# Second layer of the first two token groups in seven products instead of eight, two of them ahead of group 1's first layer

## The chip, the core and the metric

The kernel runs on one core of a Trainium2 chip. The metric is the device time of one execution in microseconds (us). TensorE (PE) multiplies matrices, VectorE (DVE), ScalarE (ACT) and GpSimd (POOL) work on tiles in SBUF (and, but for POOL, in PSUM, where products are summed), and SyncE (SP) issues the DMAs.

## The reference

Everything is fp32: causal attention of 4 batches, 12 heads, 448 tokens and 64 values a head, whose output is the input of a two-layer network.

```python
scores = scale * np.matmul(q, k.transpose(0, 1, 3, 2))
scores = np.where(mask, -1000000000.0, scores)
scores = scores - np.max(scores, axis=-1, keepdims=True)
attn = np.exp(scores)
attn = attn / (np.sum(attn, axis=-1, keepdims=True) + 1e-09)
attn_out = np.matmul(attn, v)
...
x = np.ascontiguousarray(attn_out.transpose(0, 2, 1, 3)).reshape(B * S, H * D)
h = x @ w_in
relu6 = np.clip(h + 3.0, 0.0, 6.0)
g = h * relu6 / 6.0
return (g @ w_out).astype(np.float32)
```

x is 1792 x 768, w_in 768 x 2048 and w_out 2048 x 768.

## The kernel before

**Products.** To keep fp32 exactness, both factors of a product are split into a rounded high part and the remainder. ACT casts the high part (`wh`, `gh`, line 284), and DVE or POOL subtracts it to get the remainder (`wl`, `gl`, line 296). A 128 x 128 x 448 product is then three matmuls (`triple`, lines 668 to 670): high by high, high by low, low by high.

**Groups.** The 1792 tokens are four groups of 448. Group 0 holds the first 112 queries of every batch (`first_pair`, one call for each of 6 pairs of heads). The others are computed by `unit(g, p)`: q by k (line 507), maxima on DVE (line 555, each followed by a read of its accumulator), exp on ACT (line 562), normalisation by `prow` (lines 574, 575 and 582), transposes (line 594) with their copies (lines 284 and 287), and the product with v (line 529). In the first `N_RAW` = 7 units q and k go into PE as fp32; in the later ones they are split first.

**The network.** `group(g)` does groups 0 and 1. The first layer has 16 chunks of 128 hidden rows with 18 matmuls each. Line 697 gates a chunk, and its split into `gh` and `gl` (one buffer of all 16 chunks for each) follows at once. The second layer has 6 output tiles of 16 chunks by 3 matmuls, 576 matmuls for both groups. Group 0 also turns the weights (64-bit words) into fp32: three DVE bit operations (lines 642, 644, 647), twice 384 wide for a chunk of w_in and once 512 wide for one of w_out. The result is stored in DRAM (`kept`) for the later groups.

Groups 2 and 3 are multiplied together, with seven products of halves in place of eight (`last_first`, `last_second`). This needs sums of blocks of the weights (`sums4`, `last_sums`, stored in `kept_s`) and of the activations.

**Order.** Every operation is recorded with a due time (`T_*`, `flow.op`) and with the engines that may do it. `Flow.run` then goes through the work with a cost for each operation and writes down the order of every engine; buffers, banks and the turn on one SBUF port that DVE and POOL share in this model (`port`) hold operations back. On the chip each engine goes through its list in that order and waits on semaphores. The due times in question:

```python
T_FIRST, T_EARLY, T_EACH, T_LATE, T_DENSE, T_LOAD, T_W, T_WLOAD = -66, 8, 13, 84, 7, -24, 9, 9
t = T_EARLY + T_EACH * at if g == 1 else T_LATE + T_DENSE * (at - NPAIR)
```

Of the kernel before, what the change touches and what calls it, by code (L numbers as in the profile page):

```python
# [18 lines left out]
C = 112  # L19
# [209 lines left out]
def tile_causal_attention_hardswish_moe(ctx: ExitStack, tc: tile.TileContext, q, k, v, w_in, w_out, out):  # L229
# [47 lines left out]
    def elem(n, psum=False):  # L277
        return (n + 150) / 960
# [62 lines left out]
    def first_pair(p):  # L341
        t = T_FIRST + 7 * p
        for a, src in enumerate((q, k)):
            dma(
                -900 + 4 * p, 265e3, lambda a=a: by_batch(ap(first_qk)[:, 2 * p + a]),
                lambda src=src: src[:, p, :, :, :C].rearrange("b e d s -> (e d) b s"),
                w=[(first_qk, p, a)],
            )
        dma(
            -900 + 4 * p + T_V, 265e3, lambda: ap(first_v)[:C, p].rearrange("c (b m) -> c b m", b=B),  # L350
            lambda: v[:, p, :, 0].rearrange("b c e d -> c b (e d)"), w=[(first_v, p)],
# [16 lines left out]
        def products():  # L368
            qa, ka = (by_batch(ap(first_qk)[:, 2 * p + a]) for a in range(2))
# [7 lines left out]
        pe(t, [(1.1, products, keys)], [(first_qk, p, 0), (first_qk, p, 1)], True)  # L377
# [61 lines left out]
        def times_v():  # L439
            va = ap(first_v)[:C, p].rearrange("c (b e d) -> c b e d", b=B, e=2)  # L440
# [659 lines left out]
```

## Time and profile before

| | |
|---|---|
| time, median of 3 runs | 613.1 us (612.42 to 614.92) |
| the profiled execution | 614.25 us, span 612.5 us |
| mean granted clock of TensorE | 0.989 |
| PE busy | 599.6 us (98%) |
| DVE busy | 470.2 us (77%) |
| ACT busy | 365.9 us (60%) |
| POOL busy | 269.1 us (44%) |

The span runs from the first to the last instruction of the profiled execution; its own time is 1.75 us longer. A busy share is over the whole span, whose stages differ. A row's duration on PE and DVE can overlap the next row's, so the step from one start to the next is the cost of an instruction in a row of them.

### The profile page before, as it was taken

Reading aid. Unit: us, or ns where it says so; the run is one execution under the profiler, and the core shown is the slowest. Engines: PE = TensorE matmul, PEld = TensorE weight load, DVE = VectorE, ACT = ScalarE, POOL = GpSimd, SP = SyncE. Lnnn points to the kernel's source line nnn. Section 1 sums busy time; section 2 is a strip of 40 time slices with the busy share of each in tenths; the row PEclk is TensorE's granted clock in tenths of the full one; section 3 lists DMA queues with packets and bytes.
Section 4 is the critical chain, followed back from the end, with each engine's and each line's share of the span. In section 5 each row is a group of like instructions: output and inputs, shape, how many; then the busy total and the mean of one; then the engine's idle time right before and its main releaser. Section 6 shows DMA issues by size and latency. Waiting matters only on the chain.

```text
span 612.5 us, 11307 instructions
## 1 busy us (share of the span) xinstructions
PE 599.6 (98%) x3724; PEld 522.2 (85%) x3724; DVE 470.2 (77%) x1044; ACT 365.9 (60%) x846; POOL 269.1 (44%) x277
## 2 busy tenths in 40 slices
PE   7799999999999999999999999999999999999997
PEld 5577888887888888888888888899999999999996
DVE  5879987887796876688786755588778878898861
ACT  3955757655555767776576655375545575446630
POOL 1767785654676347655184161005554343010000
PEclk8979999999999999999999999999999999999999
DMA  9969986988898654444365344435554367583321
GB/s 207 258 176 331 336 270 229 331 254 287 262 289 255 196 172 143 138 137 142 109 173 166 118 127 133 126 117 176 166 167 162 121 196 241 164 261 114 116 68 54
DMA packets 79738, 114.68 MB, mean 187 GB/s; under 512 B 20736, under 2 KB 55488, under 8 KB 79680
## 3 DMA queue, kind: packets, MB, share of 16 engines
q1 hardware_dynamic: 79248, 113.80, 61.2%
q8 instruction: 29, 0.48, 0.3%
q14 instruction: 29, 0.24, 0.1%
q10 hardware_dynamic: 432, 0.17, 0.1%
HBM read 86.80 MB, written 27.13 MB: 186 GB/s over the span
## 4 chain that ended last, share of the span: by engine, by line
PE 92%; DMA 2%; DVE 2%; ACT 2%; POOL 1%; SPq 1%; issue 0%; DVEq 0%; POOLq 0%
PE b L668 24%; PE b L669 23%; PE b L670 23%; PE b L594 7%; PE b L507 7%; PE b L529 7%; DMA gh<-in_k_dram 1%; SPq L275 1%; DMA wd<-in_w_in_dram 1%; PE b L430 1%; ACT d L284 0%; PE b L373 0%; ACT d L392 0%; POOL d L582 0%; POOL d L421 0%
## 5 line engine op out<-in xcount | busy, mean ns | idle before, releaser
L668 PE MATMUL b<-d,wh 128*128 128x448 f32 x504 | 187.4, 372 | 1.0 <-DVE r L697 1.0
L669 PE MATMUL b<-d,wh 128*128 128x448 f32 x504 | 182.9, 363 | 0.0
L670 PE MATMUL b<-d,wl 128*128 128x448 f32 x504 | 182.2, 361 | 0.0
L284 ACT CAST wh<-wd 128x768 fp32r<-128x768 f32 (+1 forms) x92 | 71.5, 778 | 59.1 <-PE b L669 35.2
L668 PEld LDWEIGHTS b<-d,wh 128*128 128x128 f32 x504 | 94.7, 188 | 10.0 <-DVE r L697 1.4
L670 PEld LDWEIGHTS b<-d,wl 128*128 128x128 f32 x504 | 94.4, 187 | 7.0 <-POOL wl L296 0.3
L669 PEld LDWEIGHTS b<-d,wh 128*128 128x128 f32 x504 | 94.8, 188 | 5.0
L555 DVE CUSTOM_DVE_ANT_0 b<-b,mask 112x448 f32<-112x448 f32 (+2 forms) x144 | 69.5, 533 | 29.8 <-PE b L507 29.1
L296 DVE TENSOR_TENSOR wl<-wd,wh 128x768 fp32r<-128x768 f32 (+1 forms) x67 | 59.9, 894 | 32.3 <-ACT wh L284 31.4
L668 PE MATMUL b<-gh,wh 128*128 128x448 f32 x192 | 74.6, 388 | 0.0
L296 POOL TENSOR_TENSOR wl<-d,wh 128x512 fp32r<-128x512 f32 (+1 forms) x38 | 58.5, 1540 | 30.0 <-ACT wh L284 28.7
L670 PE MATMUL b<-gh,wl 128*128 128x448 f32 x192 | 69.7, 363 | 0.0
L669 PE MATMUL b<-gl,wh 128*128 128x448 f32 x192 | 69.7, 363 | 0.0
L296 POOL TENSOR_TENSOR wl<-wd,wh 128x768 fp32r<-128x768 f32 (+1 forms) x25 | 43.5, 1741 | 59.1 <-DVE vr L948 43.5
L284 ACT COPY d<-b 112x336 f32<-112x336 f32 (+2 forms) x110 | 46.5, 454 | 35.5 <-PE b L594 22.1
L562 ACT ACTIVATE pr<-b,prow 112x336 f32<-112x336 f32 (+1 forms) x96 | 47.0, 497 | 9.6 <-DVE prow L555 6.3
L507 PE MATMUL b<-d 64*112 64x448 f32 (+2 forms) x376 | 46.7, 376 | 0.4 <-DVE prow L414 0.4
L582 POOL TENSOR_SCALAR pr<-pr,prow 112x224 f32<-112x224 f32 (+1 forms) x69 | 33.9, 503 | 29.3 <-DVE prow L575 19.7
L529 PE MATMUL b<-d,vr 112*64 112x224 f32 (+2 forms) x504 | 44.9, 329 | 0.0
L529 PEld LDWEIGHTS b<-d,vr 112*64 112x64 f32 x504 | 30.6, 137 | 15.6 <-issue 2.6
L296 POOL TENSOR_TENSOR d<-d 128x560 fp32r<-128x560 f32 (+3 forms) x19 | 28.0, 1473 | 35.9 <-PE b L507 18.3
L594 PE MATMUL b<-ident,pr 112*112 112x112 f32 x240 | 43.2, 262 | 0.0
(110 smaller groups left out, 1072.4 us busy)
## 6 DMA issues: line engine op xcount, KB each, us to landing
wd<-in_w_in_dram SPq DMA_DIRECT2D x32, 384.0 KB, 5.9
wd<-in_w_out_dram SPq DMA_DIRECT2D x24, 512.0 KB, 5.4
wd<-kept_w SPq DMA_DIRECT2D x32, 384.0 KB, 3.5
wd<-kept_w SPq DMA_DIRECT2D x84, 128.0 KB, 3.1
kept_w<-d SPq DMA_DIRECT2D x16, 384.0 KB, 6.5
kept_w<-d SPq DMA_DIRECT2D x24, 256.0 KB, 5.4
wd<-kept_w SPq DMA_DIRECT2D x24, 256.0 KB, 2.8
kept_s<-wd SPq DMA_DIRECT2D x12, 512.0 KB, 3.5
```

Source lines behind the costliest of these rows:

```text
L275: flow.op(key, {queue: (1, 0)}, [(0.1, lambda e: start(out=o(), in_=i()), w)], r, nbytes=nbytes)
L284: nc.scalar.copy(o(), i()) if scale is None else nc.scalar.mul(o(), i(), scale)
L296: (nc.gpsimd if e == "P" else nc.vector).tensor_tensor(o(), a(), b(), op)
L507: nc.tensor.matmul(ap(ps[e, i])[:C, :w], x[m, c], y[m, nq:nq + w], start=n == 0, stop=n == len(terms) - 1)
L529: nc.tensor.matmul(ap(av)[64 * e:64 * e + 64, off + nq - w:off + nq], ap(vr)[:, j, e, :], ap(ph)[:, e, o:o + w], start=(j == 0), stop=(j = ...
L555: lambda _, e=e, i=i, w=w, dst=dst, st=st: nc.vector.tensor_tensor_reduce(dst(), dst(), mask[:, S - w:], -0.125, 3.0e38, ALU.add, ALU.min, ...
L562: lambda _, e=e, i=i, dst=dst, st=st, pr=pr: nc.scalar.activation(row_of(pr, e, i), dst(), ACTF.Exp, bias=ap(st)[:, e, i:i + 1], scale=-1. ...
L582: (nc.gpsimd if w == "P" else nc.vector).tensor_scalar(x, x, ap(st)[:, e, 4 + i:5 + i], 1.0, ALU.mult, ALU.mult)
L594: nc.tensor.transpose(ap(tp)[:C, C * o:C * o + C], row_of(pr, e, i)[:, C * j:C * j + C], ident)
L668: nc.tensor.matmul(ps, ap(wh)[:, a], xh, start=start, stop=False, skip_group_check=more)
L669: nc.tensor.matmul(ps, ap(wh)[:, a], xl, start=False, stop=False, skip_group_check=more)
L670: nc.tensor.matmul(ps, ap(wl)[:, a], xh, start=False, stop=stop, skip_group_check=more)
```

## The change

- The second layers of groups 0 and 1 are done together by `mid_second` as seven products of 72 matmuls (504 in all). Products 1 and 2 need only group 0 and stand ahead of group 1's first layer; the other five follow it.
- The hidden values stay whole, in tiles of two chunks. `factors` makes totals and the high and low parts anew for each product, 896 wide. The sums of the weights' blocks are made earlier (`T_SUMS` 86 in place of 190).
- w_out is turned in calls of its own (`turned`, `T_OUT`), and its parts are made 768 wide from `kept`.
- Attention is due earlier (`T_EARLY`, `T_EACH`, `T_LATE`, `T_DENSE`), `N_RAW` is 9, the cost of an elementwise operation in the planner is smaller, and the pools `gh` and `gl` go into the pool `d` (38 tiles of 3.5 KB a partition in place of 22).

```diff
-T_FIRST, T_EARLY, T_EACH, T_LATE, T_DENSE, T_LOAD, T_W, T_WLOAD = -66, 8, 13, 84, 7, -24, 9, 9
-T_XA, T_X, T_LAST, T_PAIR, T_SUMS = 156, 178, 192, 10.5, 190
-N_RAW = 7
+T_FIRST, T_EARLY, T_EACH, T_LATE, T_DENSE, T_LOAD, T_W, T_WLOAD = -66, -2, 7, 40, 6.5, -24, 9, 9
+T_PRODUCT, T_PAIR = 12, 10.5
+T_GROUP = 0, 72
+T_MID = {1: 48, 2: 60, 6: 120, 7: 132, 4: 144, 5: 156, 3: 168}
+T_XA, T_X, T_LAST = 152, 168, 180
+T_OUT, T_SUMS, T_SUM = ((32, 2.5), (68, 2.5)), 86, 2.2
+N_RAW = 9
...
-    gh=1, gl=1, prow=4, r=4, kl=3, vr=3, wh=3, wl=3, pr2=3, pr1=3, wd=6, d=22,
+    prow=4, r=4, kl=3, vr=3, wh=3, wl=3, pr2=3, pr1=3, wd=6, d=38,
...
-        for m in range(NK):
-            acc, ob = bank("mo"), buf("r", [128, S])
-            for part in range(8):
...
-                    for i in (2 * part, 2 * part + 1):
-                        triple(
-                            ap(acc)[:, :n], n, wh, wl, i % 4, ap(gh)[:, i, :n], ap(gl)[:, i, :n], i == 0, i == NF - 1
-                        )
...
+    PLACE = {"11": (0, 0), "21": (0, HF), "12": (1, 0), "22": (1, HF)}
+    NAME = {1: "11", 2: "21", 6: "11", 4: "21", 7: "12", 5: "11", 3: "22"}
+
+    def factors(g, n, t0, lead=T_W + T_WLOAD):
...
+                wh, wl = parts_of(t - 6, 768, lambda wd=wd: ap(wd), [(wd, m) for m in range(HK)], HK)
+                c = 4 * hh + 2 * cc
+                ts = t0 + 1.5 * c
+                if n == 6:
+                    total(ts - 5, c, "12", "22", "12", ALU.subtract)
+                    total(ts - 4.9, c, "11", "12", "11", ALU.add)
+                elif n == 4:
+                    total(ts - 5, c, "21", "21", "11", ALU.subtract)
+                elif n == 5:
+                    total(ts - 5, c, "11", "22", "11", ALU.subtract)
+                v, (xh, xl) = gv(NAME[n], c), (buf("gt", [128, 2, S], F32R) for _ in range(2))
+                vk = [(v, 0), (v, 1)]
+                move(ts - 4.8, 2 * S, lambda xh=xh: ap(xh), lambda v=v: ap(v), vk, [(xh, 0)], {"A": 1.05})
+                minus(
+                    ts - 4.7, 2 * S, lambda xl=xl: ap(xl), lambda v=v: ap(v), lambda xh=xh: f(ap(xh)), vk + [(xh, 0)],
+                    [(xl, 0)], {"D": 1, "P": (1.87, .5)},
+                )
+                steps = [(ts + 1.5 * b, c + b, b, (xh, xl), wh, wl) for b in range(2)]
+                rows.append(steps)
+        return rows
...
+    def mid_second(g):
+        so, s1 = [buf("so", [128, 2, S]) for _ in range(HK)], [buf("kl", [128, S]) for _ in range(HK)]
+        for n, t0 in T_MID.items():
+            fresh = n in ((1, 6, 5) if T_MID[2] == T_MID[1] + T_PRODUCT else (1, 2, 6, 5))
+            if fresh:
+                X = [buf("m", [128, 512]) for _ in range(HK)]
+            for k, steps in enumerate(factors(g, n, t0, T_W + (4 if n < 3 else T_WLOAD))):
+                for ms in ([m] for m in range(HK)) if not k else [range(HK)]:
+                    row(steps, X, ms, not fresh)
...
+    for late, quarters in enumerate(((0, 1, 2, 3), (0, 2, 1, 3))):
+        for a, (x, m) in enumerate((x, m) for x in quarters for m in range(HK)):
+            t = T_OUT[late][0] + T_OUT[late][1] * a
+            turned(NF + 4 * (m + HK * late) + x, t, t - T_WLOAD)
...
-    last_sums()
+    weight_sums()
+    mid_second(both)
     last_second(last_first(last_x()))
```

The lines of the kernel after are some ten higher: a triple is at lines 676 to 678, q by k at 514, the product with v at 536, the transposes at 601, the bit operations at 640, 642 and 645, the gate at 688, the maxima at 562, a copy on DVE at 296, a subtraction or sum at 305 and a normalisation at 589.

The first place is on PE, where group 0's first layer ends. Before, transposes of attention lead into group 0's second layer, on the split hidden values `gh` and `gl`:

```order
L594 MATMUL b_1532<-ident_105,pr1_1360 112x112
L594 MATMUL b_1532<-ident_105,pr2_1303 112x112
L594 MATMUL b_1532<-ident_105,d_1212 112x112
L668 MATMUL b_1536<-gh_668,wh_1468 128x448
L669 MATMUL b_1536<-gl_686,wh_1468 128x448
L670 MATMUL b_1536<-gh_668,wl_1508 128x448
```

After, product 1 begins there, in three banks of which b_2112 is the first (b_2112 is also the first bank of product 2), on parts made by `factors` (d_705 high, d_772 low):

```order
L536 MATMUL b_2048<-d_2011,vr_1846 64x112 x4
L514 MATMUL b_2088<-d_1820 112x448
L514 MATMUL b_2090<-d_1820 112x448
L514 MATMUL b_2103<-d_1820 112x336
L514 MATMUL b_2105<-d_1820 112x336
L676 MATMUL b_2112<-d_705,wh_2063 128x448
L677 MATMUL b_2112<-d_772,wh_2063 128x448
L678 MATMUL b_2112<-d_705,wl_2079 128x448
```

On PE, 360 matmuls of triples stand from the first of the network to the first of product 2 (288 of group 0's first layer, 72 of product 1). Among them stand 64 q by k products (16 of 448 columns, 20 of 336, 28 of 224), 180 transposes, 86 products with v and 16 small matmuls of `first_pair`.

The second place is on DVE, about the middle of group 0's network. Before, bit operations on w_out (`wd`) stand between the maxima of attention:

```order
L642 TENSOR_SCALAR b<-wd 128x512
L644 SCALAR_TENSOR_TENSOR b<-wd,b 128x512
L647 SCALAR_TENSOR_TENSOR d<-wd,b 128x512
L555 ISA b,prow<-b,mask 112x448
L555 ISA prow 112x1
L642 TENSOR_SCALAR b<-wd 128x512
L644 SCALAR_TENSOR_TENSOR b<-wd,b 128x512
L647 SCALAR_TENSOR_TENSOR d<-wd,b 128x512
L555 ISA b,prow<-b,mask 112x448
```

After, four copies of transposed blocks (`d<-b`), gates and more maxima stand there as well:

```order
L296 COPY d<-b 112x336 x4
L688 SCALAR_TENSOR_TENSOR d<-r,b 128x448
L562 ISA b,prow<-b,mask 112x224
L562 ISA prow 112x1
L562 ISA b,prow<-b,mask 112x224
L562 ISA prow 112x1
L562 ISA b,prow<-b,mask 112x224
L562 ISA prow 112x1
L562 ISA b,prow<-b,mask 112x224
L562 ISA prow 112x1
L581 TENSOR_SCALAR prow<-prow 112x2x3
L582 RECIPROCAL prow<-prow 112x2x3
```

DVE's list for the stretch of PE just counted holds 30 times the three bit operations 384 wide (15 chunks of w_in) and 12 times those 512 wide, 16 gates, the 64 maxima that belong to the q by k products, 27 copies (17 of 336 columns, 5 of 224, 4 of 448, 1 of 112), 4 remainders 768 wide and 1 of 896, 5 normalisations, and 16 pairs of a small operation and a reciprocal on `prow`.

The third place is on POOL, around group 1's second layer. Before, normalisations and remainders of q and k and of w_out:

```order
L582 TENSOR_SCALAR d<-d,prow 112x448 x2
L296 TENSOR_TENSOR wl<-wd,wh 128x512
L296 TENSOR_TENSOR d<-d 128x784
L582 TENSOR_SCALAR pr_4842<-pr_4842,prow 112x224
L582 TENSOR_SCALAR pr_4817<-pr_4817,prow 112x336
L582 TENSOR_SCALAR d<-d,prow 112x448
```

After, totals and remainders of the hidden values, 896 wide, and sums of the weights (`wd<-wd`):

```order
L305 TENSOR_TENSOR d<-d 128x896
L305 TENSOR_TENSOR wd<-wd 128x256 x2
L305 TENSOR_TENSOR wl<-wd,wh 128x768
L305 TENSOR_TENSOR wd<-wd 128x256
L589 TENSOR_SCALAR d<-d,prow 112x448
L305 TENSOR_TENSOR d<-d 128x896 x6
```

In the whole program DVE and POOL go from no operation 896 wide to 72 and 25. For the stretch of PE from the chunk of group 1's first layer in bank b_3857 to the third quarter of product 7 in bank b_4633, the fourth product on PE (253 matmuls of triples, 110 transposes, 84 q by k products, 80 products with v), the lists of the two hold these operations on SBUF alone: DVE 18 of 896, 26 of 256, 9 of 768, 19 normalisations and 16 small ones; POOL 7 of 896, 10 of 256, 5 of 768, one of 784, two of 560 and 13 normalisations.

## Rows read from the trace of the kernel before

**Rows 1.** The page, parts 1 and 4: busy time and the chain that ended last.
```profile
PE 599.6 (98%) x3724; PEld 522.2 (85%) x3724; DVE 470.2 (77%) x1044; ACT 365.9 (60%) x846; POOL 269.1 (44%) x277
...
PE 92%; DMA 2%; DVE 2%; ACT 2%; POOL 1%; SPq 1%; issue 0%; DVEq 0%; POOLq 0%
```

**Rows 2.** Windows (us; PE, PEld, DVE, ACT, POOL busy; PEclk; DMA share; GB/s).
```profile
40.00:60.00 20.00, 19.01 (x99) 16.18 (x97) 17.00 (x42) 12.04 (x29) 14.42 (x13) 1.00 0.89 313
60.00:80.00 20.00, 20.00 (x127) 17.33 (x126) 19.00 (x49) 14.73 (x37) 16.40 (x16) 1.00 0.96 332
60.00:140.00 80.00, 80.00 (x488) 68.50 (x488) 68.57 (x166) 51.33 (x128) 54.82 (x54) 1.00 0.86 287
440.00:540.00 100.00, 100.00 (x501) 93.73 (x501) 82.31 (x144) 54.15 (x89) 38.70 (x32) 1.00 0.58 177
```

**Rows 3.** Timeline of PE (start us, us, engine, operation, count).
```profile
100.17 2.31 PE L529 MATMUL b<-d,vr 112*64 112x336 f32 x24
...
173.87 1.57 PE L507 MATMUL b<-d 64*112 64x448 f32 x8
...
184.62 1.20 PE L507 MATMUL b<-d 64*112 64x336 f32 x8
...
198.57 1.33 PE L507 MATMUL b<-d 64*112 64x448 f32 x12
...
207.12 1.02 PE L507 MATMUL b<-d 64*112 64x336 f32 x12
...
208.31 0.26 PE L594 MATMUL b<-ident,pr 112*112 112x112 f32 x1
208.41 0.26 PE L594 MATMUL b<-ident,d 112*112 112x112 f32 x1
```

**Rows 4.** Timeline of DVE, 70 to 113 us.
```profile
70.06 1.01 DVE L642 TENSOR_SCALAR b<-wd 128x384 int32<-128x384 int32 x2
...
72.84 0.61 DVE L697 SCALAR_TENSOR_TENSOR r<-r,b 128x448 f32<-128x448 f32 x1
...
88.98 0.63 DVE L555 CUSTOM_DVE_ANT_0 b<-b,mask 112x448 f32<-112x448 f32 x1 [1.16 <-PE b L507]
...
89.53 0.62 DVE L697 SCALAR_TENSOR_TENSOR r<-r,b 128x448 f32<-128x448 f32 x1
90.06 0.63 DVE L555 CUSTOM_DVE_ANT_0 b<-b,mask 112x448 f32<-112x448 f32 x1
...
98.80 0.43 DVE L555 CUSTOM_DVE_ANT_0 b<-b,mask 112x224 f32<-112x224 f32 x1
...
99.15 0.43 DVE L555 CUSTOM_DVE_ANT_0 b<-b,mask 112x224 f32<-112x224 f32 x1
...
110.00 0.69 DVE L642 TENSOR_SCALAR b<-wd 128x512 int32<-128x512 int32 x1
...
112.06 0.61 DVE L697 SCALAR_TENSOR_TENSOR r<-r,b 128x448 f32<-128x448 f32 x1
```

**Rows 5.** Groups of DVE instructions by shape (busy us, mean ns, idle before).
```profile
L296 DVE TENSOR_TENSOR wd<-wd 128x256 f32<-128x256 f32 x35 | 14.9, 457 | 0.9 <-DMA kept_s<-wd 0.9
...
L287 DVE COPY d<-b 112x336 f32<-112x336 f32 x21 | 10.3, 503 | 4.2 <-PE b L594 4.1
...
L296 DVE TENSOR_TENSOR d<-d 128x784 fp32r<-128x784 f32 x4 | 4.2, 1058 | 0.8 <-ACT wh L284 0.8
```

**Rows 6.** Groups of POOL instructions by shape.
```profile
L296 POOL TENSOR_TENSOR wl<-wd,wh 128x768 fp32r<-128x768 f32 x20 | 37.0, 1853 | 56.5 <-DVE vr L948 43.5 <-ACT wh L284 4.9 <-ACT d L284 2.3
...
L296 POOL TENSOR_TENSOR wd<-wd 128x256 f32<-128x256 f32 x13 | 9.5, 742 | 42.6 <-DVE wd L296 35.7 <-PE b L670 3.8 <-DVE wl L296 2.1
```

**Rows 7.** Timeline of POOL and DVE, 12 to 15 us.
```profile
12.02 1.83 POOL L421 TENSOR_TENSOR d<-d,prow 112x448 f32<-112x448 f32 x2 [10.15 <-DVE prow L414]
...
12.92 0.95 DVE L386 TENSOR_SCALAR prow<-prow 112x4 f32<-112x4 f32 x1
...
14.95 0.17 DVE L413 TENSOR_SCALAR prow<-prow 112x8 f32<-112x8 f32 x1
```

More of the change, by code (lines that the diff above doesn't have):

```diff
@@ L744, in halves @@
+                pe(t + part, [(6 * S * .4535e-3, products, [(acc, 0), ("step", t + part)])], [(wh, 0), (wl, 0)] + xs)
+            gated(t - 4, r, lambda acc=acc: ap(acc)[:, :S], (acc, 0), places[i // 2], i % 2)
+        return places
     def halves(key, x, o, v, r, ways):
@@ L774, in last_x @@
                 if h == 0:
-                    out(t, c, 1, at(0, c, 0))
-                    out(t + .2, c, 2, at(0, c, 1))
-        for k in range(5):
+                    both(t, c, (1, 2), x[0][c])
+        for k in range(3):
             for c in range(HK):
-                t = T_X + (c, 4 + c, 5.5 + c, 7 + c, 9 + c)[k]
+                t = T_X + (c, 4 + c, 5.5 + c)[k]
                 b11, b21, b12, b22 = (at(h, c, k) for h in range(2) for k in range(2))
@@ L819, in last_first @@
     def last_first(x):
-        g = [buf(a, [128, NF, S]) for a in ("gh", "gl")]
+        g = [hiddens() for _ in range(2)]
         for i in range(HF):
@@ new lines, in row, with products, store @@
+    def row(steps, banks, ms, adds):
+        def products(m):
+            for _, c, b, x, wh, wl in steps:
+                xh, xl = (ap(y)[:, b] for y in x)
+                triple(ap(banks[m])[:, :S], S, wh, wl, 2 * m + b, xh, xl, c == 0 and not adds, c == HF - 1, adds)
+        pe(
+            steps[0][0], [(len(steps) * 3 * .2013, lambda m=m: products(m), [(banks[m], 0)]) for m in ms],
+            [(y, 0) for x in steps for y in (x[4], x[5], *x[3])],
+        )
+    def store(key, g, m, o, v, queues=("SP", "SP")):
+        rows, at = by_batch(out[128 * m:128 * m + 128]), 0
+        if not g:
+            dma(key, 230e3, lambda: rows[:, :, :C], lambda: by_batch(v()), [o])
+        for (b, tiles, _), queue in zip(UNITS.get(g, ()), queues):
+            w, c = C * len(tiles), C * tiles[-1]
+            dma(
+                key, 512 * w, lambda rows=rows, b=b, c=c, w=w: rows[:, b, c:c + w],
+                lambda at=at, w=w: v()[:, at:at + w], [o], (), queue,
+            )
+            at += w
@@ L1018, in last_second @@
+            banks, rows = acc[n], factors(g, n, t0)
+            if n == 3:
+                for steps in rows[:2]:
+                    row(steps, banks, range(HK), True)
+                for m in range(HK):
+                    row([x for steps in rows[2:] for x in steps], banks, [m], True)
+            else:
+                for steps in rows:
+                    row(steps, banks, range(HK), n in (6, 7))
             t = t0 + 5
```

353 lines of the change are left out of this document (155 added, 198 removed).

## The prediction

> **What bounds the kernel now.** I read the page first: PE is busy for 599.6 of 612.5 us, and 92% of the chain that ended last is PE [rows 1]. DVE is next with 77%. So PE's own work sets the time, and a change is worth what it takes off PE, less what PE then waits for. The windows say where it waits: from 60 to 140 us PE is busy throughout, from 40 to 60 it loses 0.99 us while DVE is busy for 17.00 of 20 [rows 2]. The reader is to see two things there. A matmul taken off PE shortens the run by its full step only where nothing else is as close to the edge. And DVE is close to it early: 19.00 of 20 us from 60 to 80, 68.57 of 80 from 60 to 140, still without a wait on PE [rows 2].
>
> **What PE saves.** From 440 to 540 us PE does 501 matmuls of triples back to back in 100.00 us [rows 2], so one costs 0.1996 us. The second layers go from 576 to 504 matmuls: 72 x 0.1996 = 14.4 us less. `N_RAW` from 7 to 9 gives two units back to fp32 products. Such a unit takes 1.57 + 1.20 = 2.77 us on PE, one with split factors 1.33 + 1.02 = 2.35 [rows 3]: 2 x 0.42 = 0.84 us more. PE's net saving is 13.5 us. Moving products on PE is free in itself. It moves what the other engines owe them.
>
> **What it costs early, on DVE.** Attention is due earlier, but all of the weights' bit operations stay where they were, in group 0's network. The order gives both lists from the first matmul of the network to product 2.
>
> PE, in that stretch: 360 matmuls x 0.1996 = 71.9 us. The q by k products have 20,160 columns; the fp32 run of 1.57 us holds two of 448 and two of 336 columns, so 1.0 ns a column [rows 3], 20.2 us. Transposes start 0.10 us apart [rows 3]: 180 make 18.0. Twelve products with v (24 records) take 2.31 [rows 3]: 86 make 16.6. With 16 small ones at 0.10, 1.6, PE needs **128.3 us**.
>
> DVE, by the step from one start to the next [rows 4]: a chunk of w_in takes 72.84 - 70.06 = 2.78 us, 15 make 41.7. One of w_out takes 112.06 - 110.00 = 2.06, 12 make 24.7. A gate is 0.53, 16 make 8.5. A maximum with its read is 0.55 at 448 columns and 0.35 at 224, so about 0.45 at 336: 16, 28 and 20 make 8.8, 9.8 and 9.0. A 336-wide copy lasts 0.503 [rows 5], 0.41 as a step, since rows 4 overlap the next by some 0.09 us. With 0.54, 0.32 and 0.2 for the other widths, 27 make 11.0. Remainders 768 wide take about 0.95 (1.06 for 784 columns [rows 5], less the overlap), 5 with one of 896 make 4.9. Five normalisations at some 0.35, 1.8. Sixteen pairs of small operations, two at 0.17 [rows 7], 5.4. The sum is **125.6 us**, 98% of PE's.
>
> No row shows DVE kept at 98% by this mixture. With no gap it costs PE nothing. At the fullest slice's share, 0.95 [rows 2], DVE needs 125.6 / 0.95 = 132.2 us, 3.9 more than PE. At the average of 60 to 140, 0.857 [rows 2], it needs 146.6, or 18.3 more. In that average DVE had idle time that cost nothing, because its queue was short; here work is queued throughout. So I take **+4**, from the nearer row, 60 to 80. It can give back at most the 0.99 us that the kernel before loses from 40 to 60, since PE is busy throughout after that; I don't credit it.
>
> **What it costs late, on the port of DVE and POOL.** The hidden values' parts are now made again for each product, 896 wide, between SBUF tiles. Such operations of DVE and POOL keep each other out: while POOL works from 12.02 to 13.85 us, a DVE operation on 4 columns lasts from 12.92 to 13.87, where one on 8 columns takes 0.17 us a moment later [rows 7]. The Trainium skill's page "SBUF — State Buffer", section "Who interferes with whom", says that a VectorE instruction with two SBUF inputs and a GpSimd instruction that reads SBUF exclude each other for the whole instruction, as does a VectorE instruction in a two-port mode. By that rule the work below can't be laid side by side, and the sum is the +5 below; without it each engine alone fits under PE, and the sum is 0. The trace agrees with the rule in kind (0.95 against 0.17 us); how tightly the two can take turns it doesn't show.
>
> From group 1's chunk in b_3857 to the third quarter of product 7, PE has 253 x 0.1996 + 110 x 0.10 + 84/24 x 2.35 + 80/12 x 2.31 = 50.5 + 11.0 + 8.2 + 15.4 = **85 us**. DVE on SBUF alone, with 0.09 off each row's duration [rows 5]: 18 of 896 at 1.10 (784 columns take 1.06, so 896 about 1.19), 26 of 256 at 0.37, 9 of 768 at 0.95, 19 normalisations at no more than the 256-wide 0.37, 16 small ones at 0.14: 19.8 + 9.6 + 8.6 + 7.0 + 2.2 = 47. POOL: 1.85 for 768 columns and 0.74 for 256 [rows 6] give 2.13 for 896, 1.9 for 784 and 1.4 for 560; 7, 10 of 256, 5 of 768, one and two of those, and 13 normalisations at some 0.6 make 14.9 + 7.4 + 9.3 + 1.9 + 2.8 + 7.8 = 44. Together 91 us of 85. If operations on one engine hide wholly behind the other's, this costs 0, and no less, since PE had no wait to lose there. If the port is handed over without a gap, +6, and at a share of 0.95, +11. I take **+5**: some of the work can be done ahead, before the stretch. What is late then is the low part of a product's values, for which PE waits within products 6 and 7.
>
> **Other edits, costed at nothing.** The 36 more 128 KB loads of weights (84 to 120) and 16 more loads or stores of block sums, less the 256 KB ones of w_out, lie in or before the products, where the DMA share is about half (0.58 from 440 to 540 [rows 2]). Their cover is the lead of 13 to 18 us of due time before a product. If the early ones are late, PE waits at product 1; that is the rival on transfers. The larger pool `d` holds tiles that have no other claim. ACT has fewer operations and is at 60% [rows 1].
>
> **The sum.** The profiled execution: 612.5 - 13.5 + 4 + 5 = 608.0 us of span, and 1.75 more, as in its own time of 614.25, makes 609.8. That execution lies 1.15 above the median of 613.1 that the forecast is held against: 613.1 - 13.5 + 9 = **608.6**, say 608.5 us.
>
> **Rivals.**
> (a) All that PE saves is kept. DVE does its 125.6 us without a gap, and the port's work is spread ahead: 599.6 us, up to 602.5 with 3 us of waits. For it: PE never waits from 60 to 140 us, with DVE at 0.95 in a slice. Against it: both stretches would have to run fuller than any row.
> (b) The forecast: waits of 3 to 10.5 us together, 602.5 to 610.
> (c) The early stretch eats most of the saving: 610 to 616.2. DVE's share s decides. The saving left after the +5 is 8.5 us; 125.6 / s - 128.3 reaches it at s = 0.918. For it: from 40 to 60 us PE already waited while DVE was at 0.85 [rows 2], since a maximum or a gate can't start before its product.
> (d) Slower. The same place and mechanism, with DVE held at the share that it had on average: 18.3 us, 613.1 - 13.5 + 5 + 18.3 = 622.9. It is slower by over 0.5% below s = 0.898. For it: DVE's list is served in its written order, so a maximum that waits for its q by k products holds the bit operations queued behind it, and these are what group 0's next chunk on PE waits for. Against it: in that average PE didn't wait, so nothing pressed DVE.
> (e) Transfers, on the same side as (d). The DMA queues are at 0.96 from 60 to 80 us and at 0.86 over 60 to 140 [rows 2]. Up to 0.96 there is room for 0.10 x 80 = 8 us of transfers. If the q, k and v that are now due earlier need half as much again, 12 us by this estimate, PE loses 4 at the first units: 612.6. The stretch holds the weights' loads and stores that it held before, so I give it little.
>
> **How the numbers follow.** Chances: (a) 0.14, (b) 0.35, (c) with (e) 0.29, (d) 0.22. A measurement of this kernel tells some 0.5% from no change, 3.1 us: faster is below 610.0, slower above 616.2. Faster is (a) and (b), 0.49; the same (c), 0.29; slower (d), 0.22. The likeliest case alone runs from 602.5 to 610. The range is 600 to 621: it leaves out a few hundredths of (a), below 600, and the part of (d) at the average share and beyond, some 0.14.
>
> **What the profile will show.** PE's busy time on triples falls by 14.4 us, and q by k rises by 0.8. If the step on DVE is right, PE idles some 4 us between the first triples and product 2, ended by DVE's bit operations or gates, in slices where DVE is at 0.95 or more. If the step on the port is right, PE waits some 5 us within products 6 and 7 for a low part that DVE or POOL made, and DVE's and POOL's SBUF work together fills those slices. If instead PE idles for products of attention while DVE is at 0.86, (d) holds. I would be wrong in kind if PE waited on a DMA at product 1, or if short waits made the granted clock fall in a stretch where it is now 1.00 [rows 2], since each matmul there would then cost more than its 0.1996 us.

## The result and the profile after

The changed kernel takes 620.3 us (618.15 to 621.21, 4 runs) beside 612.9 for the kernel before: a ratio of 1.0109, 95% interval 1.0075 to 1.0144. It is slower by some 7 us where 4 faster were forecast. The profiled execution took 618.15 us, its span 616.4. It is the fastest of the four, where that of the kernel before (614.25) lies above its median, so the two spans differ by 3.9 us, some half of what the medians do. The page's busy times and chain, which answer to [rows 1]:

```profile
PE 594.1 (96%) x3636; PEld 511.2 (83%) x3636; DVE 516.8 (84%) x1039; ACT 352.7 (57%) x755; POOL 263.8 (43%) x252
...
PE 46%; DVE 12%; DMA 9%; SPq 3%; POOL 3%; issue 2%; ACT 1%; DVEq 0%; ACTq 0%; POOLq 0%
```

PE has 88 matmul records fewer, as the change says (72 of triples, 16 of two units back to fp32), but is busy for only 5.5 us less, and its idle time, span less busy, rises from 612.5 - 599.6 = 12.9 us to 22.3. PE made up 92% of the chain and now 46%; DVE, DMA and SyncE's queue (SPq) came in. The windows say where (columns as in [rows 2]); the four that answer to [rows 2], then three of 2 us, then the stretches from 40 us on:

```profile
40.00:60.00 20.00, 19.78 (x120) 15.82 (x119) 19.79 (x56) 15.54 (x40) 13.75 (x15) 1.00 0.92 317
60.00:80.00 20.00, 20.00 (x127) 15.24 (x127) 18.70 (x54) 12.39 (x32) 12.99 (x14) 1.00 0.90 315
60.00:140.00 80.00, 80.00 (x520) 62.68 (x519) 70.99 (x200) 49.41 (x133) 52.65 (x58) 1.00 0.81 262
...
440.00:540.00 100.00, 100.00 (x502) 93.75 (x501) 82.92 (x106) 55.09 (x79) 34.63 (x22) 1.00 0.29 87
...
144.00:146.00 2.00, 2.00 (x8) 1.11 (x7) 1.93 (x8) 0.64 (x2) 1.24 (x3) 0.54 0.35 135
146.00:148.00 2.00, 1.82 (x11) 1.35 (x10) 2.00 (x10) 1.30 (x5) 1.91 (x4) 0.50 0.46 103
148.00:150.00 2.00, 2.00 (x11) 1.44 (x11) 1.51 (x4) 2.00 (x7) 0.00 (x0) 0.50 0.83 223
...
40.00:140.00 100.00, 99.78 (x639) 78.50 (x638) 90.79 (x255) 64.95 (x172) 66.40 (x72) 1.00 0.84 273
140.00:200.00 60.00, 55.80 (x345) 43.26 (x344) 48.95 (x119) 32.91 (x83) 28.37 (x28) 0.94 0.80 243
200.00:280.00 80.00, 80.00 (x600) 67.04 (x600) 72.07 (x190) 53.97 (x141) 45.84 (x55) 1.00 0.89 278
280.00:420.00 140.00, 135.64 (x851) 119.31 (x852) 132.43 (x231) 80.79 (x150) 56.75 (x46) 1.00 0.66 205
```

The kernel before, in the two stretches that differ:

```profile
140.00:200.00 60.00, 60.00 (x377) 48.63 (x378) 46.60 (x112) 35.73 (x97) 37.24 (x42) 1.00 0.88 273
...
280.00:420.00 140.00, 139.79 (x967) 120.00 (x966) 99.61 (x242) 87.13 (x209) 49.85 (x60) 1.00 0.46 133
```

A matmul of a triple still takes 0.20 us (440 to 540). From 40 to 140 us PE loses 0.22 us, less than the 0.99 that the kernel before loses from 40 to 60 [rows 2], with DVE at 19.79 of 20 us in a slice. The new idle time is 60 - 55.80 = 4.20 us from 140 to 200, where the granted clock also falls to half, and 140 - 135.64 = 4.36 from 280 to 420 (before: 0 and 0.21).

The first loss, in the timeline of PE, DVE and SyncE's queue from 132 to 149 us:

```profile
132.01 0.69 DVE L645 SCALAR_TENSOR_TENSOR d<-wd,b 128x512 int32<-128x512 int32 x1
...
137.14 0.42 SPq L284 DMA_DIRECT2D kept_w<-d  x1
...
141.75 0.51 DVE L296 COPY d<-b 112x336 f32<-112x336 f32 x1 [4.27 <-DMA kept_w<-d]
...
142.31 0.41 PE L601 MATMUL b<-ident,pr 112*112 112x112 f32 x2 [1.80 <-DVE d L296]
...
143.03 2.42 PE L514 MATMUL b<-d 64*112 64x336 f32 x8
...
148.18 0.39 PE L601 MATMUL b<-ident,d 112*112 112x112 f32 x1
...
148.37 0.39 PE L601 MATMUL b<-ident,pr 112*112 112x112 f32 x1
```

DVE is not busy here but stopped: a copy of transposed blocks wants a tile of the pool `d` from which w_out is still being stored to DRAM, and waits 4.27 us. The tile was written by 132.70 us (132.01 + 0.69), but its store was issued at 137.14, behind seven other issues. The DMA engines are full when PE stops (a share of 1.02 from 140 to 142 us), but the store lands 4.5 us after its issue, no later than the median of 4.6. PE's transposes wait 1.80 us for that copy. Then the clock is at its lower level, 1.2 GHz, for some 6 us (0.54, 0.50, 0.50 in the windows), and transposes start 0.19 us apart in place of 0.10 [rows 3]. The run of fp32 products that took 1.20 us [rows 3] takes 2.42, but it starts before the clock falls and short waits stretch it, so that isn't the clock alone.

The second, further on in the same stretch (SyncE's queue, DVE and PE, 183 to 198 us):

```profile
183.42 2.69 SPq L284 DMA_DIRECT2D wd<-kept_w  x4
186.15 1.11 SPq L284 DMA_DIRECT2D d<-in_q_dram  x2
187.31 1.23 SPq L284 DMA_DIRECT2D d<-in_k_dram  x2
188.59 1.23 SPq L284 DMA_DIRECT2D d<-in_q_dram  x2
189.87 1.24 SPq L284 DMA_DIRECT2D d<-in_k_dram  x2
191.21 0.54 SPq L284 DMA_DIRECT2D wd<-in_w_out_dram  x1
...
195.75 0.69 DVE L640 TENSOR_SCALAR b<-wd 128x512 int32<-128x512 int32 x1 [2.52 <-DMA wd<-in_w_out_dram]
...
198.04 0.57 PE L601 MATMUL b<-ident,pr 112*112 112x112 f32 x4 [0.86 <-DVE d L645]
```

An issue takes SyncE 0.54 to 0.67 us here, and 12 issues of weights, q and k stand in the queue ahead of one load of w_out. DVE waits 2.52 us for that load, and the load itself takes 4.5 us from issue to landing, where the median is 6.0. PE's transposes wait 0.86 us for DVE's last bit operation: not for data of theirs but for a PSUM bank, which both use. It is the place in the queue that hurts, and not the amount: from 140 to 200 us SyncE's issues add up to 39.8 us, beside 40.2 in the kernel before.

In the late stretch PE waits within product 6 for operations between SBUF tiles: 1.25 us for a low part of values and 0.81 for one of weights. (By the count of triples product 6 runs from 329 to 352 us.) Product 7 has no wait; the other 2.3 us of the stretch are shorter waits during group 1's first layer and behind the products. The timeline of POOL, DVE and PE there:

```profile
339.42 2.09 POOL L305 TENSOR_TENSOR d<-d 128x896 f32<-128x896 f32 x1 [8.07 <-DVE d L305]
...
340.32 2.01 DVE L305 TENSOR_TENSOR wl<-wd,wh 128x768 fp32r<-128x768 f32 x1
...
343.38 0.47 PE L677 MATMUL b<-d,wh 128*128 128x448 f32 x1 [1.25 <-DVE d L305]
...
347.26 0.95 DVE L305 TENSOR_TENSOR wl<-wd,wh 128x768 fp32r<-128x768 f32 x1
...
348.26 0.47 PE L678 MATMUL b<-d,wl 128*128 128x448 f32 x1 [0.81 <-DVE wl L305]
```

DVE's operation starts 1.19 us before POOL's ends, and lasts 2.01 us where the next of its kind takes 0.95. This answers to [rows 7], with operations of the change.

### The profile page after: what moved, and what is told of

It is laid out like the page before. It is cut to its first block, busy times and chain, and to the rows that moved or that the text cites. A ratio compares the mean times of both kernels' runs of the same rounds, so it can differ in the third digit from the quotient of the medians.

```text
span 616.4 us, 10995 instructions
## 1 busy us (share of the span) xinstructions
PE 594.1 (96%) x3636; PEld 511.2 (83%) x3636; DVE 516.8 (84%) x1039; ACT 352.7 (57%) x755; POOL 263.8 (43%) x252
## 4 chain that ended last, share of the span: by engine, by line
PE 46%; DVE 12%; DMA 9%; SPq 3%; POOL 3%; issue 2%; ACT 1%; DVEq 0%; ACTq 0%; POOLq 0%
PE b L678 15%; PE b L677 14%; PE b L676 14%; DMA wd<-in_w_out_dram 3%; DVE d L305 3%; SPq L284 3%; DMA wd<-kept_w 2%; DMA kept_s<-wd 2%; DVE wl L305 1%; PE b L601 1%; DVE b L562 1%; PE b L536 1%; DVE d L296 1%; DVE wd L305 1%; DMA d<-in_k_dram 1%
## 5 line engine op out<-in xcount | busy, mean ns | idle before, releaser
L676 PE MATMUL b<-d,wh 128*128 128x448 f32 x672 | 251.2, 374 | 0.3 <-DVE d L296 0.3
L678 PE MATMUL b<-d,wl 128*128 128x448 f32 x672 | 244.6, 364 | 2.1 <-DVE wl L305 1.5
L677 PE MATMUL b<-d,wh 128*128 128x448 f32 x672 | 244.2, 363 | 1.3 <-DVE d L305 1.3
L676 PEld LDWEIGHTS b<-d,wh 128*128 128x128 f32 x672 | 126.3, 188 | 16.0 <-issue 4.4
L677 PEld LDWEIGHTS b<-d,wh 128*128 128x128 f32 x672 | 126.7, 189 | 9.5 <-DVE d L305 1.5
L293 ACT CAST wh<-wd 128x768 fp32r<-128x768 f32 x96 | 79.9, 837 | 91.5 <-PE b L677 84.3
L305 POOL TENSOR_TENSOR d<-d 128x896 fp32r<-128x896 f32 (+5 forms) x39 | 75.1, 1927 | 105.2 <-DVE wl L305 40.6
L305 DVE TENSOR_TENSOR wl<-wd,wh 128x768 fp32r<-128x768 f32 x70 | 73.1, 1045 | 28.1 <-ACT wh L293 27.0
L305 DVE TENSOR_TENSOR d<-d 128x896 fp32r<-128x896 f32 (+3 forms) x82 | 93.8, 1164 | 1.4 <-ACT d L293 1.1
L305 POOL TENSOR_TENSOR wl<-wd,wh 128x768 fp32r<-128x768 f32 x26 | 47.9, 1843 | 79.9 <-ACT wh L293 61.9
L293 ACT CAST d<-d 128x896 fp32r<-128x896 f32 (+3 forms) x78 | 70.3, 909 | 3.2 <-POOL d L305 0.9
L569 ACT ACTIVATE pr<-b,prow 112x224 f32<-112x224 f32 (+1 forms) x96 | 46.7, 493 | 16.6 <-DVE prow L562 10.7
L514 PE MATMUL b<-d 64*112 64x448 f32 (+2 forms) x360 | 48.6, 386 | 0.0
L536 PE MATMUL b<-d,vr 112*64 112x224 f32 (+2 forms) x504 | 45.8, 333 | 0.0
```

The costliest lines, as they stand in the source:

```text
L293: nc.scalar.copy(o(), i()) if scale is None else nc.scalar.mul(o(), i(), scale)
L305: (nc.gpsimd if e == "P" else nc.vector).tensor_tensor(o(), a(), b(), op)
L514: nc.tensor.matmul(ap(ps[e, i])[:C, :w], x[m, c], y[m, nq:nq + w], start=n == 0, stop=n == len(terms) - 1)
L536: nc.tensor.matmul(ap(av)[64 * e:64 * e + 64, off + nq - w:off + nq], ap(vr)[:, j, e, :], ap(ph)[:, e, o:o + w], start=(j == 0), stop=(j = ...
L569: lambda _, e=e, i=i, dst=dst, st=st, pr=pr: nc.scalar.activation(row_of(pr, e, i), dst(), ACTF.Exp, bias=ap(st)[:, e, i:i + 1], scale=-1. ...
L676: nc.tensor.matmul(ps, ap(wh)[:, a], xh, start=start, stop=False, skip_group_check=more)
```

## The experiments

Three theories. **Late weights:** the loss from 140 to 200 us comes from w_out's loads and stores, late in SyncE's queue. **DVE full:** the bit operations and attention are too much for DVE early, as the prediction's slower rival had it. **Port:** the loss after 280 us comes from wide operations of DVE and POOL keeping each other out. Where an experiment says that order is kept, the plan is that of the changed kernel and only what is emitted differs. Ratios are to the kernel before, with 95% intervals.

**Fewer transfers.** A transfer whose target is False is not issued, and the last of each set (three loads of a product's weights, two halves of q or of k) carries the bytes of all.

```diff
-        flow.op(key, {queue: (1, 0)}, [(0.1, lambda e: start(out=o(), in_=i()), w)], r, nbytes=nbytes)
+        flow.op(key, {queue: (1, 0)}, [(0.1, lambda e: o() is not False and start(out=o(), in_=i()), w)], r, nbytes=nbytes)
...
-                            t - lead, 131e3, lambda wd=wd, m=m: ap(wd)[:, m],
-                            lambda chunk=chunk, cc=cc: kept[chunk, :, 256 * cc:256 * cc + 256], [("kept", chunk)],
-                            [(wd, m)],
+                            t - lead, 131e3, lambda wd=wd, m=m: m == HK - 1 and ap(wd),
+                            lambda chunk=chunk, cc=cc: kept[
+                                chunk - 4 * HK + 4:chunk + 1:4, :, 256 * cc:256 * cc + 256
+                            ].rearrange("m p n -> p m n"), [("kept", chunk)], [(wd, m)],
...
-                        t + T_LOAD, 256 * n, lambda x=qk, h=h, c1=c1, n=n: ap(x)[64 * h:64 * h + 64, c1:c1 + n],
-                        lambda e=h, src=src, c0=c0, n=n, b=b: src[b, p, e, :, c0:c0 + n],
+                        t + T_LOAD, 256 * n, lambda x=qk, h=h, c1=c1, n=n: h == 1 and ap(x)[:, c1:c1 + n],
+                        lambda src=src, c0=c0, n=n, b=b: src[b, p, :, :, c0:c0 + n].rearrange("e d s -> (e d) s"),
```

> The changed kernel with the same bytes in fewer transfers, and the planned order of all other work kept: the three 128 KB loads of a product's weights become one of 384 KB, and the two half loads of q and of k become one each (433 issues in place of 553). Late-weights theory: the 7.2 us that PE loses between 140 and 200 us beyond the kernel before come from w_out's loads and stores being late in SyncE's queue, where an issue takes some 0.4 to 0.6 us, so the loss falls to 3 us or less and the time from 620.3 to 613 to 617 us. DVE theory (the early stretch is too full for DVE, whatever the transfers do): no change, 618 to 622.

Measured: 613.7 us, ratio 1.000 (0.9976 to 1.0024), 1.1% less than the changed kernel. Its windows:

```profile
140.00:200.00 60.00, 57.99 (x379) 46.18 (x378) 51.66 (x131) 35.45 (x90) 31.46 (x31) 1.00 0.81 269
280.00:420.00 140.00, 135.50 (x828) 119.44 (x824) 132.76 (x228) 80.32 (x145) 54.03 (x42) 1.00 0.61 194
```

The early loss falls to 2.01 us, the clock stays at its upper level, and PE does 379 matmul records in place of 345. DVE's waits for w_out's loads (4.7 us) and for its store (4.3) are gone from its list of waits. The late loss stays at 4.50. So the time in SyncE's queue held the weights back, as late weights has it. The edit makes transfers larger as well as fewer, but the traces tell the two apart: the store that stopped DVE was issued 4.44 us after the last write of its tile, and here 0.03 us after it, while from issue to landing the 24 stores of w_out take 4.5 us (median) in place of 4.6.

**One of three bit operations left out.**

```diff
             elif step == 1:
+                if m == 512:
+                    return
```

> The changed kernel with the second of the three bit operations on w_out left out (so the sign bits of w_out are lost); order and transfers stay. DVE has 24 x 0.7 = 17 us less to do while w_out is converted. DVE theory: PE's waits between 140 and 200 us go with it, 612 to 615 us. Late-weights theory: DVE waits for the loads and stores all the same, at most 2 us are gained, 618 to 621, and DVE's longest waits between 140 and 200 us still end with a transfer of w_out.

Measured: 621.4 us, ratio 1.0129 (1.0069 to 1.0189), with DVE busy 14 us less. DVE full falls for the early stretch.

**Narrow totals.**

```diff
-            minus(t, 2 * S, lambda: ap(o), lambda: ap(a), lambda: ap(b), [(a, 0), (a, 1), (b, 0), (b, 1)], [(o, 0), (o, 1)], {"D": 1, "P": (1.87, .5)}, op)
+            few = lambda x: lambda: ap(x)[:, :, :16]
+            minus(t, 2 * S, few(o), few(a), few(b), [(a, 0), (a, 1), (b, 0), (b, 1)], [(o, 0), (o, 1)], {"D": 1, "P": (1.87, .5)}, op)
```

> The changed kernel with the 16 totals of hidden values in products 6, 4 and 5 done on 16 of their 448 columns a chunk (so their products are wrong); order kept. It takes about 16 x 1.1 us of 896-wide work off the SBUF port of DVE and POOL after product 2. Port theory: PE's waits between 280 and 420 us, some 5 us more than before, fall to 2 or less, 615 to 617.5 us. If those waits come from anything else (transfers of weights, DVE's work on PSUM): 619 to 621.

Measured: 615.7 us, ratio 1.0050 (1.0024 to 1.0077). PE's idle time from 280 to 420 us falls from 4.36 to 2.28 us, by its window:

```profile
280.00:420.00 140.00, 137.72 (x869) 120.67 (x867) 120.75 (x244) 84.84 (x161) 48.74 (x50) 1.00 0.67 211
```

The wide operations are the late loss, or half of it; whether through the port or DVE's list this can't tell. The profiled execution is the slowest of the ten (620.02 us) and loses 2.64 us from 40 to 60, where the changed kernel loses 0.22, so only its late stretch is read.

**Products 1 and 2 behind group 1's first layer.**

```diff
-T_FIRST, T_EARLY, T_EACH, T_LATE, T_DENSE, T_LOAD, T_W, T_WLOAD = -66, -2, 7, 40, 6.5, -24, 9, 9
+T_FIRST, T_EARLY, T_EACH, T_LATE, T_DENSE, T_LOAD, T_W, T_WLOAD = -66, -2, 7, 70, 6.5, -24, 9, 9
...
-T_GROUP = 0, 72
-T_MID = {1: 48, 2: 60, 6: 120, 7: 132, 4: 144, 5: 156, 3: 168}
+T_GROUP = 0, 48
+T_MID = {1: 96, 2: 108, 6: 120, 7: 132, 4: 144, 5: 156, 3: 168}
```

> The changed kernel with products 1 and 2 behind group 1's first layer (group 1 due at 48, products 1 and 2 at 96 and 108) and attention of groups 2 and 3 due 30 later, without which its tiles don't fit. w_out is due at the same times but first needed some 58 us of PE time later. Late-weights theory: a late load or store now holds no product; PE's losses between 140 and 200 us fall to about 3 us and the time to 612 to 617. DVE theory: the same bit operations stand in the same stretch and still press it, 618 to 623.

Measured: 663.0 us, ratio 1.0804 (1.0755 to 1.0852), which neither theory had. Two of its windows:

```profile
240.00:260.00 20.00, 14.10 (x46) 11.20 (x47) 15.27 (x35) 7.47 (x16) 12.79 (x10) 0.67 0.89 272
260.00:280.00 20.00, 8.73 (x44) 6.79 (x43) 12.24 (x37) 5.63 (x15) 4.15 (x2) 0.67 0.76 233
```

PE stands idle for up to 11 of 20 us with no other engine full, and its longest waits are one of 7.7 us for a copy on DVE and three, 10.5 in sum, for high parts of weights. Where products 1 and 2 stood, PE had work that needed nothing of group 1. The run moved attention of groups 2 and 3 too, so it says little on either theory.

**Both edits,** the first and the third diff in one kernel.

> Both edits at once: fewer transfers and the 16 totals on 16 columns (whose products are wrong). If the two losses are of different work in different stretches, the gains add: 6.6 + 4.6 from 620.3, 608 to 611 us, and PE waits less than 2 us from 280 to 420 us. If the narrow totals gained by something that the fewer transfers already gave, 612.5 to 614.

Measured: 609.9 us, ratio 0.9948 (0.9929 to 0.9967). The gains add: 1.1% and 0.6% singly, 1.6% together. Two losses, then, in two stretches. From 280 to 420 us PE still idles for 2.71 us, where less than 2 was expected.

**POOL's wide operations on DVE.**

```diff
-            (nc.gpsimd if e == "P" else nc.vector).tensor_tensor(o(), a(), b(), op)
+            (nc.gpsimd if e == "P" and n < 896 else nc.vector).tensor_tensor(o(), a(), b(), op)
```

> The kernel with fewer transfers, in which the operations 896 wide that the plan gives to POOL are done by DVE at the same place of the order, 25 of them. Each then takes some 1.1 us in place of 2.1. Port theory: the time in which one engine holds the port falls by about 1 us for each, PE's waits from 280 to 420 us fall to 2 us or less, and the time goes from 613.7 to 610 to 612.5. If DVE's own list is what is full there, it gets 25 x 1.1 us more and PE waits longer: 615 to 622.

Measured: 616.4 us, ratio 1.0060 (1.0036 to 1.0083), slower than with fewer transfers alone. DVE's groups by shape, of the changed kernel and then of this one:

```profile
L305 DVE TENSOR_TENSOR wl<-wd,wh 128x768 fp32r<-128x768 f32 x70 | 73.1, 1045 | 28.1 <-ACT wh L293 27.0
...
L305 DVE TENSOR_TENSOR d<-d 128x896 fp32r<-128x896 f32 x48 | 59.2, 1238 | 0.7 <-ACT d L293 0.6
```

```profile
L305 DVE TENSOR_TENSOR d<-d 128x896 fp32r<-128x896 f32 x65 | 73.1, 1127 | 0.6 <-ACT d L293 0.6
L305 DVE TENSOR_TENSOR wl<-wd,wh 128x768 fp32r<-128x768 f32 x70 | 67.0, 957 | 30.9 <-ACT wh L293 30.2
```

And its window of the late stretch:

```profile
280.00:420.00 140.00, 134.47 (x819) 117.91 (x816) 131.81 (x236) 78.94 (x143) 33.76 (x31) 1.00 0.61 194
```

Without POOL's wide operations beside them, DVE's own are shorter (1238 to 1127 ns, 1045 to 957), which is the port's part. But from 280 to 420 us DVE is busy as long as before, for it does the others too, and PE idles for 5.53 us, 1.03 more than with fewer transfers alone. Another 2.1 us are lost from 40 to 140 us, where PE is busy for 97.77 in place of 99.89. The port alone as the late bound falls: DVE's list is full as well.

**Narrow maxima.**

```diff
-                            dst(), dst(), mask[:, S - w:], -0.125, 3.0e38, ALU.add, ALU.min, ap(st)[:, e, i:i + 1]
+                            *[dst()[:, :16]] * 2 if g > 1 else [dst()] * 2,
+                            mask[:, S - w:S - w + 16] if g > 1 else mask[:, S - w:], -0.125, 3.0e38, ALU.add, ALU.min, ap(st)[:, e, i:i + 1]
```

> The kernel with fewer transfers, in which the maxima of groups 2 and 3 (96 of 144, between some 130 and 330 us) look at 16 columns only, so that masking and maxima are wrong there; order kept. They read and write PSUM and don't hold the port with POOL; DVE has some 30 us less to do. If PE's waits from 280 to 420 us (4.5 us with fewer transfers) come from DVE's list being full, they fall to 2.5 or less and the time from 613.7 to 609 to 612. If they come from the port alone, they stay at 4 to 5 us: 612.5 to 614.5.

Measured: 610.9 us, ratio 0.9965 (0.9944 to 0.9987) beside 1.000, in the band of DVE's list; but PE's idle time from 280 to 420 us is 5.02, not less. The gain lies elsewhere, so this doesn't settle the late waits.

**Copies on ACT.**

```diff
-    def move(key, n, o, i, r, w, ways=None, scale=None):
+    def move(key, n, o, i, r, w, ways=None, scale=None, act=False):
...
-            if e == "A":
+            if e == "A" or act:
...
-                [(tp, 0)], [(ph, e)], {"A": 1, "D": (1, TP_LAG)},
+                [(tp, 0)], [(ph, e)], {"A": 1, "D": (1, TP_LAG)}, act=g > 1,
```

> The kernel with fewer transfers, in which the copies of transposed blocks that the plan gives to DVE in groups 2 and 3 are done by ACT at the same place of the order; the output is whole. ACT has a third of its time free from 280 to 420 us. If DVE's list is what PE waits for, 610 to 613 us; if the waits are of wide operations between SBUF tiles, which this leaves, 613 to 615; if ACT's own order then holds casts back, 615 to 620.

Measured: 610.3 us, ratio 0.9947 (0.9929 to 0.9966), with the whole output. It is faster than both kernels. Its windows:

```profile
140.00:200.00 60.00, 59.11 (x392) 48.03 (x392) 49.21 (x123) 40.38 (x107) 33.35 (x33) 1.00 0.84 275
280.00:420.00 140.00, 136.65 (x819) 120.45 (x818) 130.86 (x212) 86.83 (x162) 52.53 (x42) 1.00 0.62 191
```

PE's idle time falls from 2.01 to 0.89 us and from 4.50 to 3.35. So copies that stood in DVE's list behind other work were part of what PE waited for.

**Everything off DVE at once.** The edits of fewer transfers, narrow totals and narrow maxima, and one of three bit operations left out.

> The kernel with fewer transfers and everything that was taken off DVE alone before, at once: totals on 16 columns, maxima of groups 2 and 3 on 16 columns, the second bit operation on w_out left out (so products, maxima and w_out are wrong). DVE has some 65 us less to do, PE's work is the same. PE's work alone would give 612.9 - 13.5 = 599.4 us. If DVE's load is what keeps the rest of the saving away (609.9 with totals narrow): 602 to 606. If the rest is elsewhere (the start, copies on ACT, POOL's normalisations, transfers): 607 to 610.

Measured: 607.6 us, ratio 0.9919 (0.9887 to 0.9952), with DVE busy for 440.4 of 606.0 us, less than in the kernel before. That is the band of "elsewhere": 8.2 us above what PE's work alone would give.

**Smaller runs.** Only the products' loads made fewer, so without the last part of the first diff, that of q and k:

> The changed kernel with only the products' weights loaded in one transfer for three, q and k as before (505 issues in place of 553, 433 with both). If time in SyncE's queue is what is short from 140 to 200 us, the 48 issues saved, 12 or so of each 24 in that stretch, give a part of the 6.6 us: 615 to 618. If the wait hangs on the products' loads alone: 613 to 615.

617.0 us, ratio 1.0067 (1.0043 to 1.0091): a part of the gain, so the issues of q and k count too, and not these loads alone. Fewer transfers in the kernel before, with the lines of the first diff at its `last_second` and `unit`:

> The kernel before with the same transfers made fewer (products' weights of groups 2 and 3 one for three, q and k one for two), order kept. It has no wait of PE after 60 us, so fewer issues have nothing to give back: 611.5 to 613. If fewer issues shorten any kernel of this kind by 6 us, 606 to 608, and the gain seen in the changed kernel says nothing about the change.

612.3 us, ratio 0.9987 (0.9971 to 1.0003): no difference, so the gain answers to a loss that the change made. W_out's loads due earlier:

```diff
-            turned(NF + 4 * (m + HK * late) + x, t, t - T_WLOAD)
+            turned(NF + 4 * (m + HK * late) + x, t, t - 15)
```

> The kernel with fewer transfers, w_out's loads due 15 ahead of their bit operations in place of 9 (planned anew). Late-weights theory: the 2.0 us that PE still loses from 140 to 200 us are the rest of it and go: 611 to 613 us. If what is left there is not the loads (stores, banks, attention): 613 to 616.

Attention due later:

```diff
-T_FIRST, T_EARLY, T_EACH, T_LATE, T_DENSE, T_LOAD, T_W, T_WLOAD = -66, -2, 7, 40, 6.5, -24, 9, 9
+T_FIRST, T_EARLY, T_EACH, T_LATE, T_DENSE, T_LOAD, T_W, T_WLOAD = -66, 0, 9, 50, 6.5, -24, 9, 9
```

> The kernel with fewer transfers, attention due later and more thinly: first unit at 0 in place of -2, 9 apart in place of 7, groups 2 and 3 from 50 in place of 40 (planned anew). If early attention crowds the queue and DVE while w_out is turned, the losses from 140 to 200 us shrink and the time is 609 to 613. If group 1's first layer then waits for attention, as in the kernel with products 1 and 2 behind it, 616 to 630.

The fewer transfers told to the planner:

```diff
-                    for m in range(HK):
-                        chunk = NF + 4 * (m + (HK if n == 4 else 0)) + (0 if n == 1 else 2) + hh
...
+                    chunk = NF + 4 * (HK if n == 4 else 0) + (0 if n == 1 else 2) + hh
+                    dma(
+                        t - lead, 393e3, lambda wd=wd: ap(wd),
...
-                for h in range(2):
+                dma(
+                    t + T_LOAD, 512 * n, lambda x=qk, c1=c1, n=n: ap(x)[:, c1:c1 + n],
```

> The changed kernel with the fewer transfers written as such, so that the planner knows them and makes a new order. If the gain of 6.6 us is that of the transfers, it stays within what a new order changes: 611 to 617 us. If the planner, now seeing transfers as cheaper, puts work earlier than DVE can do it, 617 to 622.

These three took 617.8 us (1.0084, 1.0065 to 1.0102), 621.5 (1.0142, 1.0126 to 1.0158) and 625.5 (1.0205, 1.0189 to 1.0222), all slower than with the order kept. Each has a new order of all work, and waits in places where the kept order has none (in the third, 4.90 us of PE idle from 200 to 280). A new plan alone moves the time by as much as the edits do, so these three say nothing on the theories. Two more steps on top of the copies on ACT, those of group 1 as well, and two in one for the loads of the sums:

```diff
-                [(tp, 0)], [(ph, e)], {"A": 1, "D": (1, TP_LAG)}, act=g > 1,
+                [(tp, 0)], [(ph, e)], {"A": 1, "D": (1, TP_LAG)}, act=True,
```

```diff
-                    t - 4, 131e3, lambda wa=wa, j=j: ap(wa)[:, j],
+                    t - 4, 131e3, lambda wa=wa, j=j: j % 2 == 1 and ap(wa)[:, j - 1:j + 1],
```

> The kernel with fewer transfers and all copies of transposed blocks on ACT, those of group 1 too; the output is whole. In the early stretch DVE kept up with PE at 0.94 to 0.99 of its time without a wait, so taking copies off it there should change little, 609.5 to 611. If ACT is already close to what PE waits for early (it makes exp and the weights' high parts), 611 to 615.

> The kernel with fewer transfers and copies of groups 2 and 3 on ACT, and the loads for the sums of w_out's blocks two in one (24 issues fewer, 409); the output is whole. If SyncE's queue still holds something from 140 to 280 us, 607.5 to 609.5; if the three loads in one and q and k were enough, 609.5 to 611.

They took 609.8 us (0.9933, 0.9906 to 0.9959) and 610.0 (0.9949, 0.9934 to 0.9964): no difference from 610.3 that can be measured. Early copies on DVE cost nothing that shows, and neither do these 24 issues.

## Why the prediction was wrong

**The step that failed is "Other edits, costed at nothing".** It laid the transfers under the DMA share and the lead in due time. The share doesn't show the two things that were late: the time SyncE needs to issue (12 issues of weights, q and k from 183.42 to 191.21 us, 0.65 us each, ahead of one load of w_out) and the time until a store gives its tile back. Fewer issues of the same bytes gave 1.1%, 6.6 us of 620.3, for which the sum had 0. The forecast gain was 613.1 - 608.5 = 4.6 us, so this term alone turns its sign. The clock's fall is part of it: the prediction named that as a sign of being wrong in kind, and gave it no price. The rival on transfers had the right side but the wrong reason and place: it looked at the DMA share at 60 to 80 us, and priced 4 us of transfer time at the first units. That 620.3 lies within the range, and in the band of the slower rival (d), is luck: (d) has DVE's list held by a maximum that waits for its products, and what stopped PE was a copy in that list that waited for a store.

**PE's saving** was right in its count (72 matmuls at 0.20 us, 16 records of q by k fewer), but PE's busy time fell by 5.5 us, not 13.5. By the steps from one record to the next, without idle time, triples take 14.2 us less in sum (431.9 in place of 446.1), but transposes 4.9 more, q by k 2.1, where 0.8 were forecast, and products with v 2.0. Matmuls at the lower clock and short waits inside a run count as busy.

**The early cost on DVE, +4,** was too high. Loaded to 19.79 and 18.70 of 20 us in the slices from 40 to 80, DVE cost PE 0.22 us up to 140. One error was to take the fullest slice seen as the most that DVE can do. Another is PE's sum. The 125.6 us of DVE were near enough: it is busy for 129.3 from the first triple at 34.9 us to product 2 at 176.4. But PE's 128.3 were too few: with the copies on ACT, where it idles for 0.33 us in that stretch, PE is busy for 134.4, since a triple among attention's matmuls steps 0.218 us and not 0.1996. So DVE had more cover than the sum gave it. Of the 2.6 us that PE idles there in the changed kernel, 1.80 are the wait behind the store. The slower rival falls with it: 14 us less of bit operations changed nothing (621.4).

**The late cost, +5,** was nearly right in size: PE idles 4.2 us more from 280 to 420 us. The place was half right: 2.06 us are waits for low parts in product 6, and none in product 7. So was the mechanism. The Trainium skill's page "SBUF — State Buffer", section "Who interferes with whom", has such operations exclude each other for a whole instruction. The trace agrees: 2.01 us beside POOL, 0.95 alone. But the sum of both engines' work was not what decided: with POOL's part done faster on DVE, PE waited longer.

**The sum.** 613.1 - 13.5 + 9 was forecast. From 612.9, the median beside the result, PE's saving alone gives 599.4, and 620.3 was measured, so 20.9 us were lost in place of 9. Shown: 6.6 by SyncE's queue, and by ratios 0.6% or some 3.6 by the totals. The copies on ACT give back 0.5%, 3.2 us. What stays open is 7 to 8 us: with fewer transfers, narrow totals and DVE less busy than in the kernel before the time is 607.6, and PE's work alone would give 599.4. The profile of that run puts some of it into PE's idle time (606.0 - 590.0 = 16.0 us, beside 12.9 in the kernel before) and some into the transposes, whose steps add up to 48.6 us beside 45.8. What holds PE there no run separates.

## What to carry to other kernels

Count the issues of a queue as work of an engine, at the step its timeline shows, and ask for each transfer what stands ahead of it in that queue; the DMA share says little on that (0.80 in the stretch that lost most, 0.88 in it before). A saving on a full engine is kept only where every list served in order beside it has slack at the new place, so look at what an in-order wait holds up: here a copy waiting for a store stopped PE, and after it the clock. When a planner makes the order, change what is emitted and keep the plan, or the new order hides the effect.

## What the hardware showed that was not expected

DVE was busy 19.79 of 20 us without a wait of PE that mattered. One wait of PE of 1.80 us was followed by some 6 us at the lower clock, where transposes started 0.19 us apart in place of 0.10; a wait of 1.25 us at 343 us was not. A store's tile stood written for 4.44 us before SyncE came to issue the store. And transposes waited 0.86 us for a bit operation whose result they don't use, because both take their banks from one pool.
